# An attention block with an MLP gate on one core: the MLP in chunks of 512 tokens and two parts of its inner features, one PSUM bank shared earlier, and tanh at another place in ScalarE's queue

## The chip, the core and the metric

The kernel runs on one core of one Trainium2 chip. The metric is the device time of one execution in microseconds (us); lower is better. "Before" is the kernel without the change, and the profile is one execution of it, taken by the hardware profiler. The engines are named as the profile names them: PE is TensorE's matmul, PEld its weight load, DVE is VectorE, ACT is ScalarE, POOL is GpSimd, and SP is SyncE, whose queue issues nearly all DMAs.

## What is computed

One sequence of 2048 tokens, 512 features, 32 heads of 16 features, an MLP with 1792 inner features, everything in float32:

```python
xn = layernorm(x)
q, k, v = heads(xn @ wqkv)                   # 32 heads, 16 features each
p = softmax(q @ k.T * 16 ** -0.5)
s = concat(p @ v) @ wo
h = relu(xn @ w1 + b1) ** 2                  # B_w1: 512 x 1792
g = silu(h @ w2 + b2)                        # B_w2: 1792 x 512
out = x + s * g
```

## The kernel before, in words

**Numbers in two pieces.** PE multiplies in a reduced float32 format, so each operand is split into a high and a low part (`split`, L109 to L116: two POOL instructions), and one product becomes three (high by high, high by low, low by high: `terms3`, L323). Each of these products is cut once more along its 128 contraction rows into two "lanes" of 64 rows. The two halves of the PE array work on two lanes at the same time, and a "round" is one instruction, or a few, on each half.

**Attention.** The 32 heads are taken in 32 units: four heads by 512 queries each. A unit has 16 steps (in the code `st`, "slots" here, 512 in all). Per slot there are four matmuls of scores for the row maximum, 24 slots ahead (`max_mm`, L388; DVE reduces each 128x512 bank, L405), four for the exponentials (`exp_mm`, L1389; ACT writes the result, L1411), and the product with the values, which comes two slots or more behind in "visits" (`pv_visit`, L1615, matmuls at L484, 8 instructions in the profile for each slot).

**The MLP beside it.** PE's order is written out by hand. The MLP's matmuls fill the other half of the array while one half does attention. A "block" (`block`, L266) is 12 units for lane 0 and then 12 for lane 1; `long_slots` (L1768) runs it over four slots in 28 rounds. By a written pattern, 4 of these rounds hold attention on both halves and 24 hold attention on one and the MLP on the other. The pattern visits the values after rounds 12, 16 and 28, with 1, 1 and 2 slots of work, which the profile shows as bursts of 8, 8 and 16 matmuls. A burst of 16 therefore ends each block. A second form (`halves`, L228, run by `slot`, L1697) takes one slot at a time.

**Chunks.** Tokens go through the MLP in 8 chunks of 256 (`CW`). For each chunk come 7 blocks of the first product (`first_pair`, L614): two groups of 128 inner features each, so 24 units of matmul per lane and 256 columns per matmul, into the two halves of one PSUM bank. At their end ACT applies relu to the two halves (L649), and POOL squares and splits (L652, L653) into `hT`, which holds all 1792 inner features of the chunk. Then come 7 blocks of the second product (`second`, L658) with 512 columns per matmul; where the two token tiles meet, one block holds the end of one and the start of the next and uses the pattern "mixed". The split w2 stays in SBUF whole (`w2t`). The split w1 is written to DRAM in the first chunk (`w1_d`) and read back in the other seven, four DMAs of 256 KB per block (`load_part`, L590). In the first chunk the second product takes the short form for 16 slots.

**The gate.** A finished tile `u` gets b2, and four slots later `gate` (L678) issues tanh on ACT (L680), two POOL instructions and a store to `g_d`, which the last stage reads.

**Banks.** PSUM has 8 banks: the MLP holds one, and the others go round by a planner that knows how long each reader takes (`flow_take`, `flow_give`, `READERS`). From unit 4 to unit 27 (`PARTS`) the bank of the values' product is one of the planner's: each visit's sum is copied out by ACT (L1646) and added by POOL (L1647). In units 0 to 3 that bank (`po`) is kept for a whole unit and read once, six banks go round, and the pattern is "apart" instead of "shared". ACT, DVE, POOL and SP run in the order in which the program issues, and so an instruction that waits holds up all behind it on its engine.

Of the kernel before, what the change touches and what calls it, by code (L numbers as in the profile page):

```python
# [29 lines left out]
CW = 256  # L30
NCK = S // CW
VW = DH + 1
# [27 lines left out]
PARTS = range(4, 28)  # L60
# [11 lines left out]
def kernel(  # L72
# [26 lines left out]
    w1_d = dram.tile([FO, 2, P, 2, 2, P], F32, name="w1_d")  # L99

# [28 lines left out]
    with ExitStack() as ph:  # L129
# [448 lines left out]
        def mlp_tasks(mp):  # L578
            wp = mp.enter_context(tc.tile_pool(name="w2p", bufs=1))
            hp = mp.enter_context(tc.tile_pool(name="hp", bufs=1))  # L580
            up = right(wstk, "up", 1)
            m1 = ExitStack()
            rp = m1.enter_context(tc.tile_pool(name="rp", bufs=1))
            rs = [rp.tile([P, 2, CW], F32, name=f"r{i}") for i in range(2)]
# [3 lines left out]
            rot["w1s"] += [wr.tile([P, 2, 2, P], F32R, name=f"w1s{i}") for i in range(4, 8)]  # L588

            def load_part():  # L590

                if state["part"] == 2 * FO:
                    return
                fo, n = divmod(state["part"], 2)
# [8 lines left out]
            def load_w2(fo, n):  # L603
                raw = ring("ex")
                nc.sync.dma_start(raw, w2[fo * P : (fo + 1) * P, :])
                later(n, lambda: split((w2t[:, 0, fo], w2t[:, 1, fo]), raw))

            def load_xc(c):
                    xc = xp.tile([P, 2, KO, CW], F32R, name="xc")
                    for i in range(2):  # L610
                        nc.sync.dma_start(xc[:, i].bitcast(F32), xn_d[i, :, :, c * CW : (c + 1) * CW])
                    state["xc"] = xc

            def first_pair(c, f):  # L614

                if f == 0:
                    state["hT"] = hp.tile([P, 2, FO, CW], F32R, name="hT")
                if c == 0:
                    for fo in (2 * f, 2 * f + 1):
                        if fo + 2 < FO:  # L620
                            split_w1(fo + 2)

                    for n, k in ((1, 2 * f + 5), (2, 2 * f + 6)):
                        if k < FO:
                            later(n, lambda k=k: load_w1(k))
                        elif k - FO < 5:
                            later(n if f < 6 else n - 1, lambda k=k: load_w2(k - FO, 2))
                xc, hT, r = state["xc"], state["hT"], rs[f % 2]
                ps = state["pd"]
                mms = []  # L630
                for i in range(2):
                    w = state["w"].pop(0)
                    mms += terms3(ps[:, i * CW : (i + 1) * CW], [
                        (
                            lambda a, q, ko=ko, w=w: w[ko // 2][q, a, ko % 2],
                            lambda b, q, ko=ko: xc[q, b, ko],
                        )
                        for ko in range(KO)
                    ])

                out_, lh, rh, _, last = mms[3 * KO]
                mms[3 * KO] = out_, lh, rh, False, last

                between = {k: load_part for k in (2, 5, 8, 11)} if c else {}

                def post():
                    for i in range(2):
                        fo = 2 * f + i
                        nc.scalar.activation(  # L649
                            r[:, i], ps[:, i * CW : (i + 1) * CW], AF.Relu, bias=b1_t[:, fo : fo + 1]  # L650
                        )
                    nc.gpsimd.tensor_tensor(r, r, r, op=ALU.mult)  # L652
                    fs = slice(2 * f, 2 * f + 2)  # L653
                    split((hT[:, 0, fs], hT[:, 1, fs]), r)

                return block(mms, 2, post, between)

            def second(c, tt):  # L658
                hT = state["hT"]
                ps = state["pd"]  # L660
                if c and tt:
                    ps = [None]
                u = None
                th = rs[tt].rearrange("p a b -> p (a b)")
                ts_ = slice(tt * P, (tt + 1) * P)

                if c == 0 and tt == 0:
                    for k in range(5, FO):
                        later(k - 5, lambda k=k: load_w2(k, 2))

                def post():
                    nonlocal u
                    u = up.tile([P, D], F32, name="u")
                    nc.scalar.activation(u, ps[0] if c and tt else ps, AF.Copy)
                    nc.gpsimd.tensor_tensor(u, u, b2_t, op=ALU.add)
                    later(4, gate)

                def gate():  # L678
# [5 lines left out]
                    later(4, lambda: nc.sync.dma_start(g_d[t0 : t0 + P, :], u))  # L684

                mms = terms3((lambda: ps[0]) if c and tt else ps, [
                    (lambda a, q, fo=fo: hT[q, a, fo, ts_], lambda b, q, fo=fo: w2t[q, b, fo])
                    for fo in range(FO)
                ])
                if c:  # L690
                    if not tt:
                        for k in range(0, 36, 12):
                            yield from block(mms[k : k + 12], 1, None)
                        state["rest"] = mms[36:], post
                        return
                    old = state["pd"]
                    ends, end = state["rest"]

                    def take():
                        mine = [spot for spot in spots if spot[1] is pos["shared"]]  # L700
                        spots[:] = [spot for spot in spots if spot[1] is not pos["shared"]]
                        state["pd"] = ps[0] = flow_take("m")
                        spots.extend(mine)

                    def give():
                        end()
                        flow_give(old, "s")

                    yield from block(ends + mms[:6], 1, None, over=(take, give))
                    for k in range(6, 42, 12):  # L710
                        yield from block(mms[k : k + 12], 1, post if k == 30 else None)
                    return
                if c == tt == 0:
                    yield from halves(mms, (6,) * 7, post, 1)
                    return

                if tt:
                    to_block.append(1)
                    yield from halves(mms[:6], (6,), None, 1)
                    to_block.clear()  # L720
                    mms = mms[6:]
                for k in range(0, 36, 12):
                    yield from block(mms[k : k + 12], 1, post if tt and k == 24 else None)
                if not tt:
                    yield from halves(mms[36:], (6,), post, 1)

            state["pd"] = pd.tile([P, 512], F32, name="pd_t")
            state["xc"] = rot["ka"][3].rearrange("p (i k n) -> p i k n", i=2, k=KO)
            for _ in range(2):
                yield [], None  # L730
            for c in range(NCK):
                for f in range(FO // 2):
                    yield from first_pair(c, f)
                if c + 1 < NCK:

                    later(0 if c else 16, lambda c=c: load_xc(c + 1))
                    state["part"] = 0
                    for k in range(8):
                        later(13 + k, load_part)
                else:  # L740
                    m1.close()
                    wo_setup()
                for tt in range(CW // P):
                    yield from second(c, tt)
# [24 lines left out]
        def wo_pools():  # L769
# [11 lines left out]
            more += [pool.tile([P, 512], F32, name=f"xr{i}") for i in range(NXR)]  # L781
# [639 lines left out]
        def spill(c, k):  # L1421
            n = CW if c == 0 else 0
# [79 lines left out]
        for k in range(2):  # L1502
            nc.sync.dma_start(
                rot["ka"][3].rearrange("p (i k n) -> p i k n", i=2, k=KO)[:, k].bitcast(F32),
                xTs[0][:, k, :, :CW].bitcast(F32),
# [92 lines left out]
        pos = {}  # L1598

# [15 lines left out]
        def pv_visit(st, n, hold=False):  # L1615
# [21 lines left out]
            if kb == 0:  # L1637
                if u % 2:
                    pos["sum"] = sp.tile([P, 512], F32, name="ot", bufs=1)
                else:  # L1640
                    pos["sum"] = rot["ex"][0]
                nc.scalar.activation(pos["sum"], po, AF.Copy)
            else:
                rot["ex"][1:] = rot["ex"][:0:-1]
                part = rot["ex"][1]
# [51 lines left out]
        def slot(st, mms, post):  # L1697

            g = st + LEAD
# [16 lines left out]
            if st in TWO:  # L1716

                for _ in range(2):
                    max_mm(lane)
                    ex.pop(0)()  # L1720
                if ex and st < RUN - 2:
# [46 lines left out]
        def long_slots(st0, units, post, kind):  # L1768

            if not spots:  # L1770
                flow_start((pe, "se", "s", 3), (pm, "pm_t", "m", 3))
# [14 lines left out]
            for r in range(len(order) - 4):  # L1786
# [17 lines left out]
                if r + 1 in QUARTERS:  # L1804
                    max_end(st + LEAD)
                    shift_due(st + 1 + LEAD)
                if r + 1 in visits:
# [28 lines left out]
        for st_ in range(NU * 16):  # L1836
# [3 lines left out]
            if st_ == FIRST:  # L1840
                qs.close()
            item = next(dn, None)
# [57 lines left out]
```

## Time and profile before

| | before |
|---|---|
| time, three runs | 1593.82, 1594.68, 1593.82 us (median 1593.82) |
| the profiled execution | 1591.69 us, span from first to last instruction 1589.9 us |
| PE, PEld busy | 99%, 61% of the span |
| DVE, ACT, POOL busy | 84%, 80%, 47% |
| granted TensorE clock | 0.999 |
| HBM read and written | 148.90 MB and 56.34 MB |

The profiled execution's own time is 1.8 us more than its span, and 2.1 us less than the median of the three runs. Times of instructions are from the start of the span. "a<-b" says what is written from what; the text after a "<-" in brackets or at the end of a row tells what ended the idle time before the instruction.

### The profile page before, as it was taken

Reading aid. Unit: us, or ns where it says so; the run is one execution under the profiler, and the core shown is the slowest. Engines: PE = TensorE matmul, PEld = TensorE weight load, DVE = VectorE, ACT = ScalarE, POOL = GpSimd, SP = SyncE. Lnnn points to the kernel's source line nnn. Section 1 sums busy time; section 2 is a strip of 40 time slices with the busy share of each in tenths; the row PEclk is TensorE's granted clock in tenths of the full one; section 3 lists DMA queues with packets and bytes.
Section 4 is the critical chain, followed back from the end, with each engine's and each line's share of the span. In section 5 each row is a group of like instructions: output and inputs, shape, how many; then the busy total and the mean of one; then the engine's idle time right before and its main releaser. Section 6 shows DMA issues by size and latency. Waiting matters only on the chain.

```text
span 1589.9 us, 36834 instructions
## 1 busy us (share of the span) xinstructions
PE 1572.4 (99%) x13660; PEld 972.5 (61%) x13660; DVE 1342.9 (84%) x2307; ACT 1266.9 (80%) x2516; POOL 749.8 (47%) x779
## 2 busy tenths in 40 slices
PE   8999999999999999999999999999999999999998
PEld 7799765566556655665566556655665566545553
DVE  7487888888889998889888888898889989887765
ACT  7212787778888888888888888888988888888886
POOL 6437666335434533553355335533553355445521
PEclk9999999999999999999999999999999999999999
DMA  8977556535332434433433334433542263337655
GB/s 286 259 233 234 173 171 161 143 84 134 88 106 80 126 75 104 121 105 82 110 106 107 83 94 126 122 79 82 132 128 62 61 163 77 69 87 227 226 176 183
DMA packets 164178, 209.23 MB, mean 132 GB/s; under 512 B 59136, under 2 KB 79360, under 8 KB 162432
## 3 DMA queue, kind: packets, MB, share of 16 engines
q1 hardware_dynamic: 163856, 206.63, 46.5%
q8 instruction: 108, 1.77, 0.5%
q14 instruction: 70, 0.57, 0.1%
q10 hardware_dynamic: 144, 0.26, 0.0%
HBM read 148.90 MB, written 56.34 MB: 129 GB/s over the span
## 4 chain that ended last, share of the span: by engine, by line
PE 96%; DMA 2%; DVE 1%; ACT 1%; issue 0%; SPq 0%; DVEq 0%
PE po L484 12%; PE pm_t L484 10%; PE se L1399 9%; PE se L484 8%; PE pd_t L272 8%; PE pm_t L1399 8%; PE pm_t L398 6%; PE se L398 6%; PE pm_t L272 5%; PE se L272 5%; PE pm_t L1268 4%; PE po L1399 3%; PE pd_t L240 2%; PE pd_t L398 2%; PE pd_t L1268 1%; PE pm_t L240 1%
## 5 line engine op out<-in xcount | busy, mean ns | idle before, releaser
L405 DVE TENSOR_REDUCE mx<-se 128x1 f32<-128x512 f32 x840 | 552.8, 683 | 84.6 <-PE se L398 45.2
L405 DVE TENSOR_REDUCE mx<-pm_t 128x1 f32<-128x512 f32 x812 | 534.2, 683 | 75.5 <-PE pm_t L398 58.9
L1411 ACT ACTIVATE pt<-se 128x512 f32<-128x512 f32 x832 | 481.5, 616 | 45.0 <-PE se L1399 17.7
L1411 ACT ACTIVATE pt<-pm_t 128x512 f32<-128x512 f32 x736 | 429.3, 619 | 30.9 <-PE pm_t L1399 10.7
L1399 PE MATMUL se<-qe,ka 64*128 64x512 f32 x938 | 368.4, 413 | 0.0
L398 PE MATMUL se<-ka,qm 64*128 64x512 f32 x840 | 324.7, 405 | 0.2
L398 PE MATMUL pm_t<-ka,qm 64*128 64x512 f32 x812 | 320.0, 407 | 1.0 <-DVE mx L405 0.8
L1399 PE MATMUL pm_t<-qe,ka 64*128 64x512 f32 x765 | 294.6, 413 | 0.0
L1399 PEld LDWEIGHTS se<-qe,ka 64*128 64x128 f32 x938 | 167.8, 184 | 126.5 <-ACT pt L1411 85.0
L1647 POOL TENSOR_TENSOR ot<-ot,ex 128x512 f32<-128x512 f32 x85 | 109.7, 1291 | 203.1 <-ACT ex L1646 203.1
L1399 PEld LDWEIGHTS pm_t<-qe,ka 64*128 64x128 f32 x765 | 136.3, 184 | 111.3 <-ACT pt L1411 77.6
L1647 POOL TENSOR_TENSOR ex<-ex,ex 128x512 f32<-128x512 f32 x84 | 108.5, 1291 | 190.3 <-ACT ex L1646 186.6
L484 PE MATMUL po<-pt,v 128*32 128x512 f32 x1388 | 188.6, 602 | 1.4 <-DVE mx L405 0.7
L398 PEld LDWEIGHTS se<-ka,qm 64*128 64x128 f32 x840 | 153.2, 184 | 31.7 <-DVE mx L405 19.3
L484 PE MATMUL pm_t<-pt,v 128*32 128x512 f32 x1328 | 168.4, 601 | 0.8 <-ACT pt L1411 0.8
L1411 ACT ACTIVATE pt<-po 128x512 f32<-128x512 f32 x260 | 161.7, 622 | 6.6 <-PE pd_t L272 2.5
L398 PEld LDWEIGHTS pm_t<-ka,qm 64*128 64x128 f32 x812 | 147.7, 184 | 29.4 <-DVE mx L405 15.8
L405 DVE TENSOR_REDUCE mx<-pd_t 128x1 f32<-128x512 f32 x230 | 156.7, 681 | 2.2 <-PE pd_t L398 1.5
L484 PE MATMUL se<-pt,v 128*32 128x512 f32 x1104 | 140.0, 601 | 1.6 <-ACT pt L1411 1.6
L272 PE MATMUL pd_t<-xc,w1s 64*128 64x256 f32 x1008 | 136.6, 282 | 0.0
L272 PE MATMUL pd_t<-w2t,hT 64*128 64x512 f32 x492 | 130.8, 398 | 0.0
L272 PEld LDWEIGHTS pd_t<-xc,w1s 64*128 64x128 f32 x1008 | 129.8, 187 | 0.8
(220 smaller groups left out, 3212.6 us busy)
## 6 DMA issues: line engine op xcount, KB each, us to landing
w1s<-w_d SPq DMA_DIRECT2D x196, 256.0 KB
qm<-q_d SPq DMA_DIRECT2D x384, 32.0 KB
ka<-k_d SPq DMA_DIRECT2D x96, 128.0 KB
qe<-q_d SPq DMA_DIRECT2D x384, 32.0 KB
q_d<-hl SPq DMA_DIRECT2D x16, 512.0 KB
g<-g_d SPq DMA_DIRECT2D x32, 256.0 KB
k_d<-hl SPq DMA_DIRECT2D x15, 512.0 KB
on_d<-hl SPq DMA_DIRECT2D x116, 64.0 KB
```

The costliest lines, as they stand in the source:

```text
L240: mm = nc.tensor.matmul(out_() if callable(out_) else out_, lh(r), rh(r), start=first_ and lane == 0, stop=last_ and lane == 1, skip_group ...
L272: mm = nc.tensor.matmul(out_() if callable(out_) else out_, lh(r), rh(r), start=first_ and lane == 0, stop=last_ and lane == 1, skip_group ...
L398: nc.tensor.matmul(ps, qms[u][p][64 * j : 64 * j + 64, qb * P : (qb + 1) * P], kas[qd, p][64 * j : 64 * j + 64, kc * 512 : (kc + 1) * 512] ...
L405: return nc.vector.tensor_reduce(mxs[u][:, c, kc : kc + 1], ps, axis=AX.X, op=ALU.max)
L484: nc.tensor.matmul(po[32 * j : 32 * j + 32, :], vs[qd][:, (4 * kb + j) * VW : (4 * kb + j) * VW + 32], pts[j], start=first, stop=last, ski ...
L1268: mm = nc.tensor.matmul(out_, lh(r), rh(r), start=first_ and lane == first, stop=last_ and lane != first, skip_group_check=True,)
L1399: nc.tensor.matmul(se, kas[qd, j // 2][b : b + 64, kb * P : (kb + 1) * P], qes[u][j // 2][b : b + 64, :], start=True, stop=True,)
L1411: return nc.scalar.activation(pts[j], se, AF.Exp, scale=0.25)
L1647: nc.gpsimd.tensor_tensor(pos["sum"], pos["sum"], part, op=ALU.add)
```

## The change

Chunks become 512 tokens, four in all, and a chunk takes its inner features in two parts, 8 and then 6 groups of 128.

- A block of the first product is one group by 512 tokens: 12 matmuls of 512 columns per lane where it had 24 of 256, one relu, the same POOL work per block. In the first part of the first chunk (8 blocks) it keeps two groups by 256 tokens.
- `hT` holds 8 groups by 512 tokens. After the first part, each of the four token tiles gets two blocks of the second product, is copied out by ACT into `parts` and gets b2 on POOL (`second_kept`). After the second part, two tiles share three blocks, the middle one "mixed" (`second_pair`), and POOL adds the kept part (`done`). So there are 112 blocks in both kernels; 8 are "mixed" where there were 7, and none takes the short form.
- w2 is no longer kept whole. In the first chunk it is split as before but three slots after its load, written to `w2_d` six slots after that, and read back in the three other chunks (512 KB each) into a ring of 8 tiles. w1 is read back three times, not seven.
- One `r` tile serves relu, where two took turns. The values' partial sums have three tiles of their own.
- `PARTS` is `range(28)`: units 0 to 3 share the values' bank too, and use the pattern "shared". The planner starts at slot 2.
- `gate` is put on a list, and the list is emptied just before the last visit of a block of four slots, after that block's exponentials, or at the start of a short slot.

```diff
-CW = 256
+CW = 512
+PHASES = ((0, 8), (8, 6))
-PARTS = range(4, 28)
+PARTS = range(28)
...
+            r = hp.tile([P, 512], F32, name="r")
+            parts = [hp.tile([P, D], F32, name=f"part{i}") for i in range(CW // P)]
+            rot["sum"] = [hp.tile([P, 512], F32, name=f"sum{i}") for i in range(3)]
+            hT = hp.tile([P, 2, 8, CW], F32R, name="hT")
-            w2t = wp.tile([P, 2, FO, D], F32R, name="w2t")
+            make_w2 = [wp.tile([P, 2, D], F32R, name=f"w2t{i}") for i in range(8)]
+            rot["w2"], turn["w2"], w2s = make_w2, 0, {}
...
+            def load_w2(c, fo):
+                w = w2s[fo] = ring("w2")
+                if c:
+                    nc.sync.dma_start(w.bitcast(F32), w2_d[fo])
+                    return
+                raw = us[fo % 2]
                 nc.sync.dma_start(raw, w2[fo * P : (fo + 1) * P, :])
+                later(3, lambda: split((w[:, 0], w[:, 1]), raw))
+                later(9, lambda: nc.sync.dma_start(w2_d[fo], w.bitcast(F32)))
...
+            def more_w1(fo):
+                if fo + 2 < FO:
+                    split_w1(fo + 2)
+                if fo + 5 < FO:
+                    later(1, lambda: load_w1(fo + 5))
...
+            def first(c, fo, at):
+                if c == 0:
+                    more_w1(fo)
+                ps, w = state["pd"], state["w"].pop(0)
+                mms = terms3(ps, [
+                    (
+                        lambda a, q, ko=ko: w[ko // 2][q, a, ko % 2],
+                        lambda b, q, ko=ko: xc[q, b, ko],
+                    )
+                    for ko in range(KO)
+                ])
+                def post():
+                    nc.scalar.activation(r, ps, AF.Relu, bias=b1_t[:, fo : fo + 1])
                     nc.gpsimd.tensor_tensor(r, r, r, op=ALU.mult)
+                    split((hT[:, 0, at], hT[:, 1, at]), r)
+                return block(mms, 1, post, {k: load_part for k in (5, 11)} if c else {})
...
+            def keep(ps, tt):
+                nc.scalar.activation(parts[tt], ps, AF.Copy)
+                nc.gpsimd.tensor_tensor(parts[tt], parts[tt], b2_t, op=ALU.add)
+
+            def done(ps, c, tt):
+                u = us[tt % 2]
+                th = us[2] if (tt + 1) * P == CW else r
+                nc.scalar.activation(u, ps, AF.Copy)
+                nc.gpsimd.tensor_tensor(u, u, parts[tt], op=ALU.add)
...
+                later(2, lambda: gates.append(gate))
...
+            load_xc(slice(256, 512), slice(256, 512))
...
+                for f0, nf in PHASES:
+                    for k in range(nf):
+                        later((1 if c == 0 else 2) + 3 * k, lambda c=c, f=f0 + k: load_w2(c, f))
...
+                while r + 1 == len(order) - 4 and gates:
+                    gates.pop(0)()
                 if r + 1 in visits:
                     pv_visit(pv_at, visits[r + 1], r + 1 == held)
...
             if st_ == FIRST:
                 qs.close()
+                flow_start((pe, "se", "s", 3), (pm, "pm_t", "m", 3))
```

More of the change, by code (lines that the diff above doesn't have):

```diff
@@ L656, in first_pair @@
[L656 to L664, printed above, removed]
-                ts_ = slice(tt * P, (tt + 1) * P)
[L667 to L676, printed above, removed]
+                            r2[:, i], ps[:, i * 256 : (i + 1) * 256], AF.Relu,
@@ L683, in gate @@
                     t0 = c * CW + tt * P
[L684 to L725, printed above, removed]
+                    later(3, lambda: nc.sync.dma_start(g_d[t0 : t0 + P, :], u))
@@ L780, in wo_pools @@
             pool = right(wstk, "xpr", 1)
-            more += [pool.tile([P, 512], F32, name=f"xr{i}") for i in range(NXR)]
+            more += [pool.tile([P, 512], F32, name=f"xr{i}") for i in range(NXR - 3)] + state["us"]
             more += [vs["tiles"][0][:, 512 * i : 512 * i + 512] for i in range(2)]
@@ L1421, in spill @@
         def spill(c, k):
-            n = CW if c == 0 else 0
+            n = 256 if c == 0 else 0
             nc.sync.dma_start(
@@ L1598 @@
         pos = {}
+        gates = []
         def pv_step(st, pts):
```

141 lines of the change are left out of this document (87 added, 54 removed).

## The prediction, made before the changed kernel was run

> **What bounds the kernel now.** First the page of the profile, for the engines' shares; then the stages, cut where the kind of block changes; then PE's row of instructions, for the price of one block.
>
> ```profile
> span 1589.9 us, 36834 instructions
> ...
> PE 1572.4 (99%) x13660; PEld 972.5 (61%) x13660; DVE 1342.9 (84%) x2307; ACT 1266.9 (80%) x2516; POOL 749.8 (47%) x779
> ```
> ```profile
> core 0: us, PE busy (x) PEld busy (x) DVE busy (x) ACT busy (x) POOL busy (x), PEclk, DMA share, GB/s
> 172.49:251.20 78.71, 78.71 (x789) 52.13 (x785) 69.81 (x118) 62.66 (x127) 53.95 (x79) 1.00 0.57 173
> 251.20:297.61 46.41, 46.41 (x356) 24.60 (x352) 40.15 (x68) 34.33 (x66) 29.16 (x32) 1.00 0.57 139
> 297.61:331.45 33.84, 33.84 (x269) 17.54 (x265) 30.11 (x52) 26.20 (x51) 3.66 (x5) 1.00 0.38 110
> 331.45:1408.00 1076.55, 1073.34 (x9718) 638.32 (x9714) 966.45 (x1625) 934.00 (x1868) 497.44 (x485) 1.00 0.39 101
> 1408.00:1420.00 12.00, 11.30 (x93) 6.07 (x90) 10.07 (x17) 10.18 (x20) 5.62 (x5) 1.00 0.14 35
> ```
>
> PE is busy through every stage of the MLP, at the full clock, and no other engine is over 90% in the long fourth stage (DVE 966.45 of 1076.55). So time is gained by putting less on PE, or by taking out the few places where it waits. These five stages are the whole MLP: 7 blocks of the first product in the first chunk (11.24 us each), 16 short slots (2.90 each, 11.60 for four), 3 blocks of the second product (11.28), 97 blocks from 331.45 on, and the last block. Together they take 1247.51 us for the work of 112 blocks, and the change leaves the work before and after them alone.
>
> PE's bursts of 16 value matmuls each end a block, so the distance between them is the price of a block. Between the first two rows lie six blocks of the first product, between the second and third three of the second, then one "mixed", then one of the second product again:
>
> ```profile
> 496.77 1.92 PE L484 MATMUL se<-pt,v 128*32 128x512 f32 x16 [0.18 <-ACT pt L1411]
> ...
> 563.31 1.92 PE L484 MATMUL pm_t<-pt,v 128*32 128x512 f32 x16
> ...
> 596.18 1.92 PE L484 MATMUL po<-pt,v 128*32 128x512 f32 x16
> 607.44 1.92 PE L484 MATMUL pm_t<-pt,v 128*32 128x512 f32 x16
> 618.72 1.92 PE L484 MATMUL po<-pt,v 128*32 128x512 f32 x16 [0.26 <-ACT pt L1411]
> ```
>
> Narrow block (256 columns): 66.54 / 6 = 11.09 us. Wide block (512 columns): 32.87 / 3 = 10.957. Mixed: 11.26. The last one took 11.28, 0.32 more than its kind, and its burst waited for ACT.
>
> **The change part by part. Width.** The rounds show why narrow costs more. Each pair is the first and the last of nine MLP rounds in a row, the upper narrow, the lower wide:
>
> ```profile
> 561.07 0.40 PE L272 MATMUL pm_t<-xc,w1s 64*128 64x256 f32 x2
> ...
> 562.99 0.40 PE L272 MATMUL pm_t<-xc,w1s 64*128 64x256 f32 x2
> ...
> 565.97 0.39 PE L272 MATMUL pm_t<-w2t,hT 64*128 64x512 f32 x1
> ...
> 567.84 0.39 PE L272 MATMUL pm_t<-w2t,hT 64*128 64x512 f32 x1
> ```
>
> Eight rounds take 1.92 us against 1.87: 0.240 and 0.234 each. Over the 24 MLP rounds of a block that makes 0.15, close to the 0.133 between the blocks; I take the blocks. The trace has no first product at 512 columns. A round with it has the same shapes (64 rows, 128 weights, 512 columns) as one of the second product, so 10.957 is its nearest row and 11.09 the upper bound; less than 10.957 is excluded because the attention half of a round keeps its 512 columns.
>
> **Units 0 to 3.** With six banks in turn the blocks take 11.24 to 11.28 us whether narrow or wide, and four short slots 11.60. With the pattern and the seven banks of the later units, the first chunk's 14 blocks of the first product (8 narrow, 6 wide) take 8 x 11.09 + 6 x 10.957 = 154.5 us, where the first 14 blocks' worth takes 78.71 + 46.41 + 33.84 = 158.96: 4.5 less. The evacuations that this adds are on ACT and POOL: see POOL below.
>
> **Tanh.**
>
> ```profile
> 617.53 0.65 ACT L680 ACTIVATE r<-u 128x512 f32<-128x512 f32 x1
> 618.05 0.62 ACT L1411 ACTIVATE pt<-po 128x512 f32<-128x512 f32 x1
> ...
> 620.71 0.60 ACT L1642 ACTIVATE ex<-po 128x512 f32<-128x512 f32 x1 [1.06 <-PE po L484]
> ```
> ```profile
> 576.26 0.60 ACT L1642 ACTIVATE ot<-se 128x512 f32<-128x512 f32 x1 [1.25 <-PE se L484]
> ```
> ```profile
> L680 ACT ACTIVATE r<-u 128x512 f32<-128x512 f32 x13 | 8.5, 653 | 0.0
> L674 ACT ACTIVATE u<-pd_t 128x512 f32<-128x512 f32 x5 | 3.3, 666 | 0.0
> ```
>
> Tanh holds ACT 0.52 us (617.53 to 618.05) between exponentials that the block's last visit needs, and PE's burst at 618.72 comes 0.32 late. In the fourth stage there are 13 of them: 4.2 us. Behind the last exponential ACT idles over 1 us until the burst is done (1.06 and 1.25), so a tanh put there fits, also beside the relu or copy that ends some blocks. It is moved past the exponentials alone; the two POOL instructions and the store to `g_d` that follow it feed only the last stage. Cost 0, at most 16 x 0.32 = 5.1.
>
> **The sum over blocks.** The fourth stage holds 49 narrow blocks, 7 mixed and 41 wide: 543.4 + 78.8 + 449.2 = 1071.5. It took 1076.55; tanh is 4.2 of the difference, and 0.9 is other waits that I leave in. After the change the MLP is 8 narrow, 8 mixed, 95 wide (48 of the first product), and the last block, whose pattern stays as it is: 88.7 + 90.1 + 1040.9 + 12.0 + 0.9 = 1232.6. That is 14.9 us below 1247.5: 4.5 in the first chunk's first blocks, 6.5 from width later on, 4.2 from tanh, less 0.3 for the eighth mixed block.
>
> **The rest, costed at nothing.**
>
> ```profile
> w1s<-w_d SPq DMA_DIRECT2D x196, 256.0 KB
> ```
>
> DMA: w1 is read back 28 x 3 times 256 KB where it was 196, 28 MB less; w2 adds 7 MB written and 21 MB read. The DMA share of 0.39 in the fourth stage stays, w2 tiles come many blocks ahead, and SP issues fewer instructions. If the cover were gone, a late 512 KB tile would hold PE by what it is late. The 16 kept tiles add 16 copies on ACT (0.67 each, as L674) and 16 additions on POOL; the copy stands where a block without it has ACT idle 1.25 us. Without that cover: 10.7 us. The two loads of the second half of the chunk at slot 2 go ahead of SP's loads for the next units; 1 MB at 173 / 0.57 = 304 GB/s is 3.5 us and it is needed a block (11 us) later: between 0 and 1 us, I take 0. The three u tiles now serve the last stage as buffers for exponentials; the store of the last gate must be out of one first: 0 to 2 us, I take 0, as that store is issued before.
>
> **POOL in the first chunk** is the cost I am least sure of. These are its rows between 172.5 and 251.2, then one of later visits, then one wait:
>
> ```profile
> L114 POOL TENSOR_TENSOR w1s<-ex,w1s 128x256 fp32r<-128x256 f32 x23 | 16.9, 734 | 1.9
> L113 POOL TENSOR_SCALAR w1s<-ex 128x256 fp32r<-128x256 f32 x23 | 9.3, 406 | 0.0
> L114 POOL TENSOR_TENSOR hT<-r,hT 128x512 fp32r<-128x512 f32 x6 | 7.8, 1293 | 0.5
> L652 POOL TENSOR_TENSOR r<-r 128x512 f32<-128x512 f32 x6 | 6.2, 1040 | 17.7 <-ACT r L649 17.7
> L114 POOL TENSOR_TENSOR w2t<-ex,w2t 128x512 fp32r<-128x512 f32 x3 | 3.8, 1281 | 0.2
> L113 POOL TENSOR_SCALAR hT<-r 128x512 fp32r<-128x512 f32 x6 | 3.7, 620 | 0.5
> L113 POOL TENSOR_SCALAR w2t<-ex 128x512 fp32r<-128x512 f32 x3 | 1.9, 628 | 0.0
> L536 POOL TENSOR_TENSOR ot<-ot,hl 128x512 f32<-128x512 f32 x1 | 1.3, 1287 | 3.4 <-DMA hl<-r_d 3.4
> ...
> L538 POOL TENSOR_TENSOR hl<-ot,hl 128x512 fp32r<-128x512 f32 x1 | 1.3, 1272 | 0.1
> ...
> L537 POOL TENSOR_SCALAR hl<-ot 128x512 fp32r<-128x512 f32 x1 | 0.6, 617 | 0.1
> ```
> ```profile
> L1647 POOL TENSOR_TENSOR ex<-ex,ex 128x512 f32<-128x512 f32 x84 | 108.5, 1291 | 190.3 <-ACT ex L1646 186.6 <-DMA ka<-k_d 3.6
> ```
> ```profile
> 273.52 0.62 POOL L113 TENSOR_SCALAR w2t<-ex 128x512 fp32r<-128x512 f32 x1 [3.09 <-DMA ex<-in_B_w_dram]
> ```
>
> A block of the first part will need: square and split of r 1.04 + 0.62 + 1.29 = 2.95; one group of w1, 2 x (0.41 + 0.73) = 2.28; one group of w2, 0.63 + 1.28 = 1.91; two partial sums, 2 x 1.29 = 2.58; a quarter of a unit's scaling, (1.29 + 0.62 + 1.27) / 4 = 0.80. That is 10.5 us of 11.09, 95%, where this stage had 53.95 / 78.71 = 69%. POOL keeps up with 0.6 us per block to spare, and it may run late without harm: the next relu needs the one r tile a block after the last, so 11.09 - 2.95 = 8 us. Beyond that the relu waits, and behind it on ACT stand the last visit's copy and the next exponentials, and for these PE. The six blocks of the second part need 9.8 of 10.957 (only four split w1). I take 0; the upper end is in the first rival.
>
> Against the profiled execution: 1591.69 - 14.9 = 1576.8. The median of the runs is 2.1 above that execution, so the forecast is 1593.82 - 14.9 = 1578.9 us.
>
> **The rivals. POOL is late in the first chunk.** For: 95%, and one wait of 3.4 us for a DMA in each unit (L536) would make it 11.4 per block. Against: an instruction that is late finds its input ready, so such waits shrink. With 0.3 to 1.2 us too much over 14 blocks, less the 8 us that it may lag, PE loses 0 to 9 us: about 1584, up to 1588.
>
> **POOL and SP hold each other: slower.** In the first chunk SP's load of the next w1 group waits until POOL has split an old one, the load of w2 stands behind it on SP, and POOL's split of w2 then waits for that load, as it did at 273.52. If each of the 14 splits waited 3.09 us, that is 43 us, less 0.5 spare for 14 blocks and 8 us of lag: 28 us lost, 13 slower than before: 1607. It passes no-change from 14 x W = 15 + 14.9, so W = 2.1 us. Against: a load has three slots (8 us) where before it had two, and only 5 of 14 splits waited before, 7.4 us in all.
>
> **Width is worth less.** For: in the first stages narrow (11.24) and wide (11.28) were alike, so something else in a first block, such as its relu or its loads, might cost the 0.133. Against: the rounds themselves differ. If nothing comes of it, 48 x 0.133 = 6.4 is lost: 1585.3. The Trainium skill ("TensorE: Matmul & The Clock Gate", section "Wait — 56ns, not 53.3ns?") gives a warm matmul its columns at 2.4 GHz and a fixed 2.5 ns or so, by which halving a matmul costs 2.5 ns a round and 0.06 us a block, an estimate that would put the time at 1582.4. The rows show 6 ns a round, which decides for the larger gain.
>
> **Tanh still costs.** At the end of a block it stands ahead of the copy that frees the values' bank, and if that copy comes later the planner's next bank does too. With 0.32 for each of 16: 1584.0. Against: ACT's idle time there is twice what tanh takes.
>
> **How the numbers follow.** Forecast as summed 0.64; POOL late 0.18; width 0.05; tanh 0.05; two of these three at full price, which ends near 1594, 0.03; POOL and SP 0.05. About 0.2% (3.2 us) is what a measurement of this kernel can tell from no change, so faster means below 1590.6: 0.64 + 0.18 + 0.05 + 0.05 = 0.92, the same 0.03, slower 0.05. The range goes down to 1575.5 (the 0.9 of other waits gone, the last block at 10.957, and 1.5 for what blocks and runs differ by) and up to 1586.5, which takes in width, tanh and most of the late POOL.
>
> **What would show it.** Right: 16-bursts 10.96 us apart in blocks of the first product from the first chunk's second part on, 11.09 in the eight narrow ones; no burst held by ACT behind a tanh; POOL near 95% busy in the first 89 us of the MLP with PE still at 100%; PE down by 1152 matmuls (48 blocks with 24 fewer each); the MLP 1233 us long. Wrong: PE waiting for relu or for a partial sum's copy in the first 160 us, 11.09 in wide blocks, or a last stage longer than its 170 us.

## The result and the profile after

| | before | after |
|---|---|---|
| median of the runs, us | 1593.82 (1593.33 to 1594.68, 4 runs) | 1582.41 (1582.37 to 1582.76, 4 runs) |
| ratio, 95% interval | | 0.9928 [0.9911, 0.9946] |
| profiled execution, us (span) | 1591.69 (1589.9) | 1582.42 (1580.6) |
| the MLP, us | 1247.51 | 1231.30 |
| after the MLP, us | 169.90 | 177.08 |

The kernel became 11.4 us faster by the medians; the forecast was 14.9. By the profiled executions it is 9.3, since before's profiled execution was 2.1 us under its own median and after's stands on it. The spans are compared below, because they can be taken apart: the MLP starts 0.27 earlier, takes 16.21 less, and what follows it takes 7.18 more, together 9.30 less.

The page of after, engines' shares:

```profile
span 1580.6 us, 34509 instructions
...
PE 1560.8 (99%) x12508; PEld 884.2 (56%) x12508; DVE 1342.5 (85%) x2307; ACT 1281.0 (81%) x2513; POOL 807.7 (51%) x824
```

PE has 13660 - 12508 = 1152 matmuls fewer, 48 blocks with 24 fewer each. The stages of after: eight narrow blocks, eight wide ones (the second product of the first part), the long middle, the MLP's last block, and then the first two pieces of the last stage.

```profile
core 0: us, PE busy (x) PEld busy (x) DVE busy (x) ACT busy (x) POOL busy (x), PEclk, DMA share, GB/s
172.22:260.79 88.57, 88.57 (x900) 59.33 (x897) 79.75 (x135) 78.98 (x161) 78.55 (x94) 1.00 0.67 205
260.79:348.42 87.63, 87.63 (x709) 45.65 (x705) 79.68 (x134) 75.05 (x148) 32.41 (x31) 1.00 0.29 65
348.42:1392.10 1043.68, 1043.68 (x8364) 542.31 (x8360) 946.43 (x1592) 916.28 (x1799) 530.21 (x522) 1.00 0.40 104
1392.10:1403.52 11.42, 11.33 (x93) 6.22 (x89) 9.92 (x17) 10.69 (x21) 5.21 (x5) 1.00 0.24 48
1403.52:1413.40 9.88, 9.88 (x80) 4.52 (x76) 7.80 (x15) 7.99 (x16) 4.67 (x7) 1.00 0.80 249
1413.40:1429.28 15.88, 8.78 (x58) 4.81 (x54) 5.42 (x10) 6.55 (x12) 2.58 (x2) 0.79 0.70 235
```

The first four rows are the MLP. PE is busy through the first three without a gap: 88.57 / 8 = 11.07 us per narrow block, 87.63 / 8 = 10.95 per wide one. POOL, the doubtful engine, has 78.55 of 88.57 in the first row, 89%. The sixth row is the surprise: 15.88 us in which PE worked 8.78, with a granted clock of 0.79.

Blocks of the first product at 512 columns did not exist before. Their first bursts of 16, a block apart:

```profile
346.56 1.92 PE L486 MATMUL po<-pt,v 128*32 128x512 f32 x16
357.51 1.92 PE L486 MATMUL se<-pt,v 128*32 128x512 f32 x16
368.45 1.92 PE L486 MATMUL se<-pt,v 128*32 128x512 f32 x16
379.38 1.93 PE L486 MATMUL pm_t<-pt,v 128*32 128x512 f32 x16
```

Each distance is 10.93 to 10.95, the price of a block of the second product. The wait table of PE for the long middle, where before had its ACT waits, is empty.

What happened at 1416 is told by three answers for 1400 to 1432: PE's, ACT's and SP's wait tables (what waited for what: us in total, times, the longest), then the chain of waits.

```profile
PE pd_t L242 <- ACT u L1441: 7.1, 1, 7.1
...
ACT u L1441 <- DMA g_d<-u: 7.1, 2, 5.4
...
SPq L477 <- DMA sh_d<-sh: 5.1, 1, 5.1
```
```profile
1409.18 6.86 DMA sh_d<-sh
1416.05 0.52 SPq L477
...
1419.11 3.49 DMA g_d<-u
1422.71 1.09 ACT u L1441 x2
1423.85 0.79 PE pd_t L242
```

Read backwards: PE's next slot starts at 1423.85 behind exponentials that ACT writes into a u tile; ACT waited until that tile's store to `g_d` was out; and that store was issued only at 1419.11. The next two fences show why, in SP's row of instructions and in POOL's:

```profile
1409.18 0.56 SPq L460 DMA_DIRECT2D sh_d<-sh  x1
1409.81 0.42 SPq L710 DMA_DIRECT2D g_d<-u  x1
1416.05 2.08 SPq L477 DMA_DIRECT2D qe<-sh_d  x4
...
1419.11 0.43 SPq L710 DMA_DIRECT2D g_d<-u  x1
```
```profile
1407.20 1.30 POOL L708 TENSOR_TENSOR u<-u,u 128x512 f32<-128x512 f32 x1
```

The value to be stored was ready at 1408.5. The program puts its store three slots after the gate, and by then SP's queue had reached the loads of `qe` from `sh_d`, which waited for the store of `sh` issued at 1409.18; that store took 6.86 us, at the time when DMA engines were 70 to 80% busy with the last stage's first loads. So 10.6 us passed between the value and its store. The two slots in question took 10.45 and 5.43 us (1413.40 to 1423.85 to 1429.28) where a slot of this stage takes 3.28 (1429.28 to the next at 1432.56): 9.3 lost.

### The profile page after: what moved, and what is told of

Same layout as the page of the kernel before. It is cut to its first block, busy times and chain, and to the rows that moved or that the text cites. A ratio compares the mean times of both kernels' runs of the same rounds, so it can differ in the third digit from the quotient of the medians.

```text
span 1580.6 us, 34509 instructions
## 1 busy us (share of the span) xinstructions
PE 1560.8 (99%) x12508; PEld 884.2 (56%) x12508; DVE 1342.5 (85%) x2307; ACT 1281.0 (81%) x2513; POOL 807.7 (51%) x824
## 4 chain that ended last, share of the span: by engine, by line
PE 96%; DVE 1%; DMA 1%; SPq 0%; issue 0%; ACT 0%; DVEq 0%; ACTq 0%
PE se L486 17%; PE se L1429 12%; PE po L486 9%; PE pd_t L274 7%; PE pm_t L400 7%; PE pm_t L274 7%; PE pm_t L1429 7%; PE se L400 6%; PE pm_t L486 5%; PE pm_t L1298 4%; PE po L1429 4%; PE pd_t L400 2%; PE po L400 2%; PE pd_t L1298 1%; PE pd_t L242 1%; PE pm_t L242 1%
## 5 line engine op out<-in xcount | busy, mean ns | idle before, releaser
L1441 ACT ACTIVATE pt<-se 128x512 f32<-128x512 f32 x980 | 566.9, 621 | 32.0 <-PE se L1429 10.4
L1441 ACT ACTIVATE pt<-pm_t 128x512 f32<-128x512 f32 x546 | 325.9, 620 | 8.3 <-PE pm_t L274 3.7
L486 PE MATMUL se<-pt,v 128*32 128x512 f32 x2224 | 282.1, 601 | 0.0
L1678 POOL TENSOR_TENSOR sum<-sum,sum 128x512 f32<-128x512 f32 x99 | 127.9, 1292 | 188.7 <-ACT sum L1677 188.4
L1678 POOL TENSOR_TENSOR ot<-ot,sum 128x512 f32<-128x512 f32 x99 | 127.9, 1292 | 180.7 <-ACT sum L1677 180.6
L274 PE MATMUL pm_t<-w2t,hT 64*128 64x512 f32 x780 | 206.7, 398 | 0.0
L274 PE MATMUL pm_t<-xc,w1s 64*128 64x512 f32 x672 | 177.4, 396 | 0.0
L407 DVE TENSOR_REDUCE mx<-po 128x1 f32<-128x512 f32 x201 | 137.4, 684 | 22.6 <-PE po L400 19.4
L274 PE MATMUL pd_t<-xc,w1s 64*128 64x512 f32 (+1 forms) x672 | 152.2, 363 | 0.0
L274 PEld LDWEIGHTS pm_t<-w2t,hT 64*128 64x128 f32 x780 | 139.3, 184 | 4.1
```

Of the source, the lines that this page charges most:

```text
L274: mm = nc.tensor.matmul(out_() if callable(out_) else out_, lh(r), rh(r), start=first_ and lane == 0, stop=last_ and lane == 1, skip_group ...
L407: return nc.vector.tensor_reduce(mxs[u][:, c, kc : kc + 1], ps, axis=AX.X, op=ALU.max)
L486: nc.tensor.matmul(po[32 * j : 32 * j + 32, :], vs[qd][:, (4 * kb + j) * VW : (4 * kb + j) * VW + 32], pts[j], start=first, stop=last, ski ...
L1441: return nc.scalar.activation(pts[j], se, AF.Exp, scale=0.25)
L1678: nc.gpsimd.tensor_tensor(pos["sum"], pos["sum"], part, op=ALU.add)
```

## The experiments

Each kernel ran beside runs of the kernel before on the same chip. Kernels 1 to 4 ran together (before 1592.05 there), so did 5, 6, 7 and 11 (1592.83) and 8, 9 and 10 (1592.34); differences between kernels of different groups, after among them, are taken by their ratios.

**1. The u tiles as the last buffers.** In after the three u tiles stand behind the x tiles and ahead of the older buffers in the list from which the last stage takes tiles for its exponentials. Here they go to its end, so that other tiles are written first.

```
-more += [... xr tiles ...] + state["us"]
+more += [... xr tiles ...]
...
-rot["pt"] = more + rot["pt"]
+rot["pt"] = more + rot["pt"] + state["us"]
```

> The changed kernel with the three u tiles put last in the list of buffers for exponentials, behind the 17 old ones, instead of 17th to 19th. Theory 1 (the u tiles): the changed kernel lost 7.2 us in one wait and about 2 more at a low clock in the last stage, because exponentials were sent into u tiles whose store had not left; without that the stage has no wait over 1 us at its start, and the time is 9 us below the changed kernel's: about 1573. Theory 2 (the stage's own start: SP has some 20 DMAs in 15 us there, and what is late is what they bring): another wait takes the place of this one, and the time stays within 3 us of 1582.4.

Measured: 1574.81 us (1573.84 to 1577.61), ratio 0.9887 [0.9871, 0.9902], 6.5 below after by the ratios (7.6 by the medians). The same stretch of the last stage in this kernel, in one piece:

```profile
1413.50:1428.50 15.00, 15.00 (x124) 8.79 (x122) 11.16 (x20) 12.80 (x26) 6.49 (x6) 1.00 0.72 245
```

PE is busy throughout, at the full clock. So the wait was for these tiles, and nothing else in the list has it. The profiled execution of this kernel, the slowest of its four, has a span of 1575.8, only 4.8 below after's. A part of what is missing to 9.3 is visible: PE waits for other loads later in the last stage, and behind that wait (it ends at 1490.04) the granted clock was 0.50 for 3.41 us. This is PE's wait table from 1400 on:

```profile
PE pm_t L242 <- DMA oc<-on_d: 1.7, 1, 1.7
```

Before has a wait of this kind too, of 0.5 us, and two waits for DVE of 0.8 and 0.7: 2.0 in its last stage that after does not have. Such waits differ from trace to trace (0.3 for these loads in kernel 4, none in kernel 11).

**2. The store issued at once.** The other way to end the wait: the list stays as in after, but the last gate's store is issued with the gate and not three slots later.

```
-later(3, lambda: nc.sync.dma_start(g_d[t0 : t0 + P, :], u))
+later(0 if c == NCK - 1 and tt == 3 else 3, lambda: nc.sync.dma_start(...))
```

> The changed kernel with the store of the last gate issued together with the gate, not three slots later; the u tiles keep their place in the list. Theory 1, in its form that SP's queue made the store late (it stood behind four loads that waited 5.1 us for a DMA): the store leaves about 9 us earlier, the exponentials find the tile free, and 7 to 9 us are gained, 1573 to 1576. If it is the tiles' place in the list alone that matters, or theory 2 holds: under 2 us.

Measured: 1576.41 us (1575.62 to 1577.23), ratio 0.9899 [0.9885, 0.9912], 4.6 below after by the ratios (6.0 by the medians), less than the 7 to 9 expected. SP's row: both stores now go ahead of the loads of `qe`; PE's wait table has 2.1 left of the 7.1. The last line is from the chain of waits.

```profile
1409.94 1.30 SPq L710 DMA_DIRECT2D g_d<-u  x2
1415.67 2.10 SPq L477 DMA_DIRECT2D qe<-sh_d  x4
```
```profile
PE pd_t L242 <- ACT u L1441: 2.1, 1, 2.1
```
```profile
1410.92 5.92 DMA g_d<-u
```

Most of the loss was therefore the place in SP's queue. The rest is the store's own time beside the other transfers: it took 5.92 us even when it was issued at once.

**3. Narrow first products again.** On kernel 1, the 48 wide blocks of the first product are computed as 24 pairs of matmuls of 256 columns in place of 24 of 512; the tiles and the planner's pattern stay. One of the two loads of w1 inside such a block also moves, from its sixth unit of the second lane to its ninth.

```
-mms = terms3(ps, [ ... xc[q, b, ko] ... ])
+for i in range(2):
+    cs = slice(256 * i, 256 * i + 256)
+    mms += terms3(ps[:, cs], [ ... xc[q, b, ko, cs] ... ])
...
-return block(mms, 1, post, {k: load_part for k in (5, 11)} if c else {})
+return block(mms, 2, post, {k: load_part for k in (8, 11)} if c else {})
```

> As e1_u_last, but the 48 wide blocks of the first product use 24 matmuls of 256 columns per lane (two halves of the tokens, same work, same relu, same loads). If the width is what the blocks differ by: each block goes from 10.96 to 11.09 us, 48 x 0.133 = 6.4 us more than e1_u_last. If it is something else in a narrow block (two relus, four loads): no difference. By a fixed 2.5 ns per matmul: 2.9 us.

Measured: 1581.28 us (1580.14 to 1582.54), ratio 0.9928 [0.9916, 0.9941], 6.5 above kernel 1. Six of these blocks in a row, kernel 1 and then this one, first and last burst:

```profile
346.65 1.92 PE L486 MATMUL po<-pt,v 128*32 128x512 f32 x16
...
412.36 1.92 PE L486 MATMUL se<-pt,v 128*32 128x512 f32 x16
```
```profile
346.86 1.92 PE L486 MATMUL po<-pt,v 128*32 128x512 f32 x16
...
413.38 1.92 PE L486 MATMUL se<-pt,v 128*32 128x512 f32 x16
```

65.71 / 6 = 10.95 against 66.52 / 6 = 11.09. The difference, 0.135, is 5.6 ns for each of 24 rounds. The moved load has no part in that: the six blocks shown are of the first chunk, which reads no w1 back, and PE has no wait in the MLP of either kernel. A fixed 2.5 ns per matmul, the Trainium skill's figure ("TensorE: Matmul & The Clock Gate", section "Wait — 56ns, not 53.3ns?"), would have made it 2.9 us in all, an estimate from that figure (48 x 24 x 2.5 ns); this trace does not agree with that as the price of a halved matmul in such rounds.

**4. Tanh where it was.** On kernel 1, all gates but those of the last tile of the last chunk go back to their old place, four slots after the copy.

```
-later(2, lambda: gates.append(gate))
+if c == NCK - 1 and tt == 3:
+    later(2, lambda: gates.append(gate))
+else:
+    later(4, gate)
```

> As e1_u_last, but tanh is issued four slots after its tile, between exponentials, as before the change (the last tile's stays on the list). If tanh costs what it cost before: 0.32 us at each of 15, 4.8 us more than e1_u_last, seen as bursts of 16 that wait for ACT. If the place had become harmless with one relu of 512 columns instead of two: under 1 us.

Measured: 1579.28 us (1578.31 to 1580.29), ratio 0.9917 [0.9903, 0.993], 4.5 above kernel 1. PE's wait table between 414 and 1392, empty in after, is again that of before:

```profile
PE se L486 <- ACT pt L1444: 2.0, 8, 0.3
PE pm_t L486 <- ACT pt L1444: 0.8, 3, 0.3
PE po L486 <- ACT pt L1444: 0.8, 3, 0.3
```

These are 14 waits of 0.3 us; a fifteenth, of 0.6, holds the MLP's last burst, and from its first burst to its last the MLP is 4.7 us longer than in kernel 1. That is the cost that was read in before, burst by burst.

**5. Units 0 to 3 on the old pattern.** On kernel 1, the shared bank and the later units' pattern begin at unit 4 again.

```
-PARTS = range(28)
+PARTS = range(4, 28)
```

> As e1_u_last, but units 0 to 3 keep the bank of the values' product for themselves and use the pattern 'apart', as before the change. If the seven banks and the other pattern are worth what the blocks said: the first chunk's 15 blocks in these units cost 11.24 to 11.28 us each again, 8 x 0.15 + 7 x 0.32 = 3.4 us more than e1_u_last. If the partial sums that sharing adds on ACT and POOL take it back: no difference.

Measured: 1578.53 us (1577.88 to 1579.13), ratio 0.9911 [0.9896, 0.9926]: 0.24% or 3.8 us above kernel 1. The expectation was 3.4. In the trace the sixteenth burst of 16 stands at 350.95 where kernel 1 has it at 346.65, and the difference of 4.3 stays to the MLP's end; 0.5 of it is there at the first burst (181.91 against 181.44), so 3.8 fall between the first and the sixteenth.

**6 and 7. POOL loaded with more work.** On kernel 1, each of the 14 blocks of the first product in the first chunk gets two, then four more squares of r on POOL, 1.04 us each, behind the split. The hidden values are split off before them, and nothing reads the extra results.

```
 split((hT[:, 0, fs, cs], hT[:, 1, fs, cs]), r2)
+for _ in range(2):
+    nc.gpsimd.tensor_tensor(r, r, r, op=ALU.mult)
...
 split((hT[:, 0, at], hT[:, 1, at]), r)
+for _ in range(2 if c == 0 else 0):
+    nc.gpsimd.tensor_tensor(r, r, r, op=ALU.mult)
```

> As e1_u_last, with two more POOL instructions of 1.04 us behind each block of the first product in the first chunk (they square r once more when it is no longer needed; the output stays). POOL was busy 78.6 of 88.6 us in the first part, 9.8 us a block; this makes it 11.9 against 11.07. If POOL may lag by some 8 us before PE feels it, as the prediction had it: 8 blocks x 0.85 = 6.8 us of lag, no time lost, under 1 us. If PE, through SP or a partial sum, feels any lag: 6 to 12 us more than e1_u_last.

> As e6_pool_2 with four more POOL instructions a block: POOL's need becomes 14.0 us a block against 11.07 and, in the second part, 12.3 to 14 against 10.96. If PE feels it only past 8 us of lag: 8 x 2.9 - 8 = 15 us lost in the first part and up to 10 in the second, 15 to 25 us more than e1_u_last, with PE waiting behind a relu or a partial sum's copy. If POOL's place in the chain is not what I think: either nothing, or all of 40 us.

Measured: 1587.69 us (1585.79 to 1589.36), ratio 0.9968 [0.9956, 0.998], and 1613.87 us (1612.01 to 1615.87), ratio 1.0134 [1.0117, 1.0151]: 12.9 and 39.3 above kernel 1. A POOL that may lag 8 us would have made it under 1 and 15 to 25; the second loss is nearly the 40 that its expectation names last. The head of PE's wait table of the first of them, from 172 to 430:

```profile
PE pd_t L274 <- ACT r L654: 2.9, 3, 1.4
PE se L400 <- ACT sum L1681: 2.2, 1, 2.2
```

Both an evacuation into r and the copy of a partial sum hold PE. But these two kernels hold r itself 2 and 4 us longer, so they do not say whether r or POOL's lag is to blame. Kernel 8 was made for that.

**8. Two more instructions, off r.** As kernel 6, but the two extra instructions square a constant into a tile that nothing reads at that time.

```
-nc.gpsimd.tensor_tensor(r, r, r, op=ALU.mult)
+nc.gpsimd.tensor_tensor(us[2], b2_t, b2_t, op=ALU.mult)
```

> As the run with two extra squares per block, but the two extra POOL instructions write a scratch tile that nothing reads, out of a constant, so that r is let go as soon as it is split. If that run lost 12.9 us because r was held 2 us longer in each block, this one loses 0 to 3 us against the kernel with its u tiles last (1575 to 1578). If any lag of POOL holds PE, through the partial sums that ACT copies out for POOL or through the splits of w1 and w2, it loses about the same, 9 to 14 us (1584 to 1589).

Measured: 1586.29 us (1583.83 to 1587.9), ratio 0.9957 [0.9943, 0.9972], 11.1 above kernel 1. So it is the lag, and r is not needed for it. The heads of ACT's and PE's wait tables from 225 to 425:

```profile
ACT sum L1681 <- POOL ot L1682: 10.5, 5, 3.0
...
ACT sum L1681 <- POOL sum L1682: 1.9, 1, 1.9
ACT r L680 <- POOL hT L116: 0.7, 1, 0.7
```
```profile
PE se L400 <- ACT sum L1681: 2.2, 1, 2.2
PE po L1433 <- ACT sum L1681: 1.3, 1, 1.3
```

ACT's copy of a partial sum needs a tile that POOL's addition of an earlier partial sum still holds, and PE needs the bank that this copy empties. r, on which the prediction rested its allowance, accounts for 0.7 of 13.1.

**9. One more instruction.** As kernel 6 with one extra square in place of two.

```
-for _ in range(2 if c == 0 else 0):
+for _ in range(1 if c == 0 else 0):
```

> One extra square of r per block in the first chunk in place of two. POOL has 78.55 us of work in the 88.57 us of the first eight blocks after the change, 9.82 per block of 11.07; one more instruction of 1.04 makes 10.86, which still fits. By the sum of busy times alone nothing is lost: 1574 to 1576. If POOL's waits for loads and for ACT don't shrink when it is late, it has less than that to spare, and 2 to 7 us are lost.

Measured: 1575.93 us (1574.27 to 1576.9), ratio 0.9893 [0.9879, 0.9906], 1.0 above kernel 1, which the times alone cannot tell from nothing. The trace can. Up to the seventh burst of 16 it keeps kernel 1's pace, but the eighth comes 12.45 us after it (248.01 to 260.46) where kernel 1 takes 11.09 (247.88 to 258.97). The chain is that of kernel 8; these are lines of ACT's and PE's wait tables:

```profile
ACT sum L1681 <- POOL ot L1682: 1.7, 1, 1.7
```
```profile
PE se L400 <- ACT sum L1681: 0.8, 1, 0.8
```

In after PE has no wait at all in these blocks. So after's own load on POOL stands just short of the point at which PE feels it: one more instruction per block is felt in the last of the eight blocks, by 1.4 us, and two are felt from the seventh on (13.2 and 12.95 us in kernels 6 and 8).

**10. The tanh alone, on the kernel before.** Nothing of the rest is changed: the gates go into a list and are issued behind the last exponentials of a block.

```
-later(4, gate)
+later(2, lambda: gates.append(gate))
...
+while r + 1 == len(order) - 4 and gates:
+    gates.pop(0)()
```

> The kernel before with one part of the change alone: the tanh and its gate go behind the last exponentials of a block. If each of the 13 tanh of the fourth stage cost PE 0.32 us, as the trace of before says, this is 4.2 us below before, near 1588.5. If the late tanh costs as much elsewhere (the copy that frees the bank, the next block's bank), 0 to 1 us below. If the tanh also cost something in the three stages that the trace did not show, 4.5 to 5.1 below.

Measured: 1586.92 us (1585.67 to 1588.74), ratio 0.9965 [0.9952, 0.9979], 5.4 below before (the interval is 3.3 to 7.6). In the trace 4.3 of it lie in the MLP (its last burst is 4.59 earlier than in before, its first 0.26), the rest in the last stage. PE's wait table for 414 to 1392 is empty. ACT's row around one tanh:

```profile
616.94 1.13 ACT L1411 ACTIVATE pt<-se 128x512 f32<-128x512 f32 x2
617.90 0.68 ACT L680 ACTIVATE r<-u 128x512 f32<-128x512 f32 x1
619.32 0.60 ACT L1643 ACTIVATE ex<-po 128x512 f32<-128x512 f32 x1 [0.73 <-PE po L484]
```

The tanh lies behind the exponentials and ACT still idles 0.73 us before the next copy.

**11. Both ways of ending the u wait.** Kernels 1 and 2 together.

```
-rot["pt"] = more + rot["pt"]
+rot["pt"] = more + rot["pt"] + state["us"]
...
-later(3, lambda: nc.sync.dma_start(g_d[t0 : t0 + P, :], u))
+later(0 if c == NCK - 1 and tt == 3 else 3, lambda: nc.sync.dma_start(...))
```

> e1_u_last and e2_store_early together, the version meant to be the best. If both act on the same wait, it is as e1_u_last within 1 us, about 1574 to 1575; if the early store also brings the last tile's other transfers forward, up to 1 us below.

Measured: 1573.81 us (1572.87 to 1575.48), ratio 0.9883 [0.9868, 0.9897], the fastest of all; the runs do not separate it from kernel 1. From its MLP's end to the end of the span only 0.2 us of PE waits are left in the table, and its span, 1571.1, is 9.5 below after's.

## Why the prediction came out as it did

**The MLP: right.** Forecast 1232.6 us, measured 1231.3. Its three terms hold when each is undone alone: width 6.5 forecast and 6.5 measured (kernel 3); units 0 to 3 4.5 forecast and 3.8 measured (kernel 5, which does not bring back the 16 short slots that are part of the 4.5; in after itself these 14 blocks take 88.57 + 6 x 10.95 = 154.3 where 154.5 was forecast); tanh 4.2 forecast and 4.5 measured (kernel 4, 4.7 in its trace; alone on the kernel before 5.4, of which 4.3 lie in the MLP). Two lines of the sum were too high: the last block, kept at 12.0 and now 11.42, and the 0.9 of other waits, of which 0.3 are left (87.63 + 1043.68 against 90.1 + 1040.9). Of the signs named, wide blocks 10.95 apart (10.96 forecast), narrow ones 11.07 (11.09), the missing matmuls and the bursts no longer held behind a tanh all came.

**The step that failed** is the sentence on the u tiles: "the store of the last gate must be out of one first: 0 to 2 us, I take 0, as that store is issued before". It measured 9.3 us in the profile, and 6.5 and 7.2 by the ratios of the two kernels that have none of it (1 and 11). "Issued before" was thought in the order of the program; on SP the store came 10.6 us after its value, behind loads that wait for the store of `sh`. The bound of 2 us was a bound on a transfer, and left out the queue ahead of it: the same part of the prediction looked at SP for the loads of the second half of the chunk but not for this store. It was short for the transfer too, which took 5.92 us in kernel 2. And 2.1 of the 9.3 are the slow slot behind the wait, for which the prediction had no term. The sign set for it, "a last stage longer than its 170 us", did come: 177.08.

By the spans the sum closes: forecast 1589.9 - 14.9 = 1575.0; plus 9.3 for the u tiles, less 2.1 for waits that before's last stage had elsewhere, less 1.3 in the MLP, less 0.3 at its start, is 1580.6. The medians show 3.5 of that 5.6, as before's profiled execution was 2.1 under its median. Of the 2.1 in before's last stage, 2.0 stand in its wait table; what they hang on was not tried.

That the time still came within 3.5 us of the forecast, and inside its range, is partly luck. The room upwards was made for width, tanh and POOL, and none of these used it. And kernel 1, without the failed step, is 18.0 us below before by its ratio, 3.1 more than forecast: gains that were not in the forecast, 1.3 of them in the MLP, hid a part of the loss.

**POOL in the first chunk: the answer right, one reason wrong.** 95% was forecast, 89% measured in that stage (POOL still works for some us behind it), with no loss. But "it may run late without harm" for 8 us does not hold. By the prediction's own 10.5 us per block, two extra instructions make 12.58 of 11.07: 1.5 too much, 12 us over the eight narrow blocks, of which 8 should have been free. By the tenth burst of 16 kernel 8 had lost 6.3 us against kernel 1 (287.23 against 280.88) and kernel 6 7.7 (288.58), so only about 4 to 6 were free. By POOL's measured 10.1 us per block (78.55 in the row and 2.6 behind it, over eight blocks) it is less, 1.5 to 3. In the six wide blocks of the second part, (9.8 + 2.08 - 10.957) x 6 = 5.5 us too much cost another 4.1 in kernel 8, whose burst 24 stands at 444.98 where kernel 1 has it at 434.57. The buffer that gives way first is not r but the partial sums' tiles, of which two take turns for the copies. The rival of a late POOL was thus nearer than its text had it: one instruction per block more costs about 1 us, two cost 11 to 13.

**The other rivals.** The width is not worth less (kernel 3). The tanh does not cost again elsewhere (kernel 10). That POOL and SP hold each other would have shown as PE waits in the first chunk; after has none.

## What to carry to other kernels

When a change lets a later stage reuse a tile, price the last reader of that tile by where it stands in its engine's queue and by the longest wait ahead of it there, not by its own duration; then issue that reader at once, or put the tile last in the list of buffers, which here gained more. An in-order engine that is 90% busy was harmless here only as far as the smallest buffer among all the work in its queue reached, so go through every tile that it frees, not only the one under discussion. Terms read off the distance between bursts, and waits read off single bursts, held to within 1 us here.

## What the hardware showed that was not expected

A wait of PE can cost more than its length. After the 7.1 us wait, PE's rounds stood 0.43 us apart, then 0.23 again in the slot at 1429.28:

```profile
1424.44 0.62 PE L242 MATMUL pd_t<-wot,ka 64*128 64x512 f32 x1
1424.87 0.62 PE L242 MATMUL pd_t<-wot,ka 64*128 64x512 f32 x1
...
1429.61 0.39 PE L242 MATMUL pm_t<-wot,ka 64*128 64x512 f32 x1
1429.84 0.40 PE L242 MATMUL pm_t<-wot,ka 64*128 64x512 f32 x1
```

That slot took 5.43 us in place of 3.28, 2.1 us on top of the wait. The granted clock (the third figure from the end of the next row) was 0.50 from before the wait was over:

```profile
1421.81:1428.64 6.83, 4.79 (x22) 3.00 (x26) 2.77 (x4) 3.99 (x8) 0.00 (x0) 0.50 0.96 336
```

The Trainium skill ("TensorE: Matmul & The Clock Gate", section "Part 1: The HAM clock gate (the "warmup" mystery)") says that PE goes to half its clock after an idle window of about 3.4 us and back after as much work; the trace agrees with the half pace. It shows more than that rule: in kernel 2 a wait of only 2.07 us (until 1418.54) was also followed by slow rounds, and the clock fell only 1.4 us after PE had resumed:

```profile
1420.12 0.62 PE L242 MATMUL pd_t<-wot,oc 64*128 64x512 f32 x1
...
1420.97 0.62 PE L242 MATMUL pd_t<-wot,oc 64*128 64x512 f32 x1
```
```profile
1419.95:1423.36 3.41, 3.41 (x18) 0.94 (x14) 1.97 (x4) 2.39 (x5) 0.53 (x1) 0.50 0.93 212
```

The rounds are 0.42 apart again (1420.97 - 1420.12 over two), and the slot took 4.85 us (1418.54 to 1423.39): 1.6 lost behind a wait of 2.07. Kernel 1 has the same 3.41 us at 0.50 behind its wait of 1.7, and the 6.83 of after are twice 3.41. But the longest PE waits of kernels 6 and 8, 2.2 us, were followed by no fall of the clock. So the length of a wait alone does not tell here whether it is followed by such a stretch; what else decides was not tried.
